# Two blocks of x turned on TensorE, thirds of queries taken in another order, and a rewritten order of work

## The chip, the cores and the metric

The kernel runs on one core of a Trainium2 chip. The core has TensorE (PE: matmuls and transposes; its weight loads, PEld, are shown apart), VectorE (DVE), ScalarE (ACT), GpSimd (POOL) and SyncE (SP), which here issues transfers. Each engine works through its own queue in order; engines meet through semaphores. The metric is the time of one execution in microseconds (us), taken as a median of several runs. Matmul results land in PSUM, which has eight banks of 2 KB per partition; they are copied or reduced from there by DVE or ACT.

## The reference

Attention in clusters is followed by a feed-forward layer, with 4 batches, 8 heads, 768 tokens, 64 numbers per head, and 16 centroids per head:

```python
q_assign = np.argmax(np.einsum('bhsd,hcd->bhsc', q_n, c_n), axis=-1)
k_assign = np.argmax(np.einsum('bhsd,hcd->bhsc', k_n, c_n), axis=-1)
mask = q_assign[:, :, :, None] == k_assign[:, :, None, :]
scores = np.where(mask, scale * np.matmul(q, k.transpose(0, 1, 3, 2)), -1e9)
attn = softmax(scores)
x = matmul(attn, v)              # then (B, S, H*D) -> 3072 tokens of 512
h = x @ w_in                     # 512 -> 1024
solu = h * softmax(h)
ln = (solu - mean) / sqrt(var + 1e-6) * g_ln
out = ln @ w_out                 # 1024 -> 512
```

## The kernel before

**First layer.** Work goes by pairs of heads (four pairs in each of four batches; a pair is written batch.pair). q and k of a pair are loaded and turned so that the head's numbers lie in partitions: in batch 0 by PE in fp32 (`turn_tokens`, L386, copied out by DVE or ACT at L393), later by DVE (L407). They are cast to bf16 into the pair's buffer `qk` (`cast`, L431 to L435). Centroid products (`clusters`, L445 and L450) are turned back by DVE (L459), the maximum taken (L472), the best cluster marked (L478, L484), turned (L491, L494), and the marks placed as further rows beside q and k (`place`, L506 to L514). So the score matmul adds a large constant where the clusters agree, and the exponential is taken with that constant as a shift: the mask costs no instruction.

A unit is two or three blocks of 128 queries of a head. Its scores fill three PSUM banks of 512 columns (two matmuls of 256 each, L601), or six narrower ones for pair 0.0; there are 294 banks in all and a ring of three buffers, `sps`. ACT takes the exponential of each bank into `e` (L607, nine buffers). Value matmuls (L624, six for each 128 queries) sum into one PSUM bank, `ops`. DVE divides by the sum of weights (the normalise, L636 and L649) and so writes x. There is one buffer of `ops`, so the value matmuls of a group wait for the normalise of the group before.

**Second layer.** It goes by blocks of 128 tokens, f = 0 to 23. x is turned into `xT` by a DMA transpose from SP (`turn_x`, L679), two blocks at a time in batches 0 to 2 (`turned`, L666) and one at a time after that; the last block is turned by PE into a buffer of the ring `sps` (`turn_x_pe`, L682) and copied out by DVE (`keep_x`, L690). Then PE makes h (L710, eight matmuls of 512 columns, written in four parts of two); DVE takes the negative maximum over 1024 columns (L716), ACT the exponential (L722) and DVE the product u (L727). u is turned (L732, by PE for the last two blocks), DVE takes its statistics (L738, L742), POOL makes the scale (L748 to L757), PE multiplies by w_out (L771), and ACT or DVE scales the result (L786, L788), which SP sends out (L798). One further PSUM bank, the pool `ps_m`, is passed along between the cluster products and the y of the blocks. An operation with `take="m"` waits for the `give="m"` of the one before it.

w_in comes in four loads of 512 KB (L549), each cast to bf16 by POOL (`cast_w_in`, L551; operations wi0 to wi3); h needs all four. w_out comes in four loads (L565), is multiplied by the gains and centred: weighted sums on PE (su0, su1: L574), a copy of them (sk: L581), a mean on PE (me: L584) and eight DVE instructions (L587).

**Order.** `Weave` (L16) holds all operations of a run with an engine, what they need and a cost. `ORDER` (L29 to L75) writes down for each engine the kinds of operations in sequence: S a bank of scores, E its exponential, V the values of a block, N a normalise, tp, xa, ca the turn, copy and cast of q or k, cl, tb, mx, oh, ot, pl the cluster steps, xt the turn by DVE, ld and lv loads, h, hm, ex, u, tu, bn, ag, at, al, y, sc, ou the steps of the second layer, tx the turn of x. The n-th token of a kind takes the n-th operation of that kind given to the engine; `AWAY` (L77) names operations moved from their usual engine to another. So the order in which each engine issues is fixed, and the chip's semaphores set the times.

`FIRST` (L280) is the order in which the pairs 1 to 3 of batch 0 are taken after pair 0, as (pair, third of the queries): (1,0) (1,1) (2,0) (2,1) (3,0) (3,1) and then the last third of each. The first two blocks of x need the first third of every pair.

## Time and profile before

| what | value |
|---|---|
| time, median of 3 runs | 225.78 us (225.64 to 225.80) |
| the profiled execution: time, span | 225.95 us, 223.9 us |
| PE, DVE, ACT, POOL busy | 215.1, 197.3, 191.5, 127.1 us |
| granted TensorE clock | 1.00 |
| chain that ended last | PE 86%, ACT 5%, DVE 3% |
| first h matmul, first maximum, first exponential of the second layer | 46.2, 49.0, 50.4 us |
| transposes of x by DMA, issue to landing (median) | 14, 3.2 us |
| loads of w_in, issue to landing (median) | 4, 5.9 us |

The span goes from the first to the last instruction; the rest of the time lies around it. A line of the timeline has start and duration in us, engine, line of the program, operation, output<-input, shapes and count; in brackets stands how long the engine was idle before it and what ended that. Matmuls overlap in a pipeline, so the distance from one start to the next, and not the duration, tells what one costs.

### The profile page before, as it was taken

The page shows a single profiled execution, that of the slowest core. Times are in us where ns is not written, and L with a number is a line of the kernel's source. Part 1 is how long each engine was busy: PE and PEld are TensorE (multiplying, and loading weights), DVE is VectorE, ACT ScalarE, POOL GpSimd, SP SyncE. Part 2 cuts the span into 40 slices and gives each one's busy share as a digit, 9 for nine tenths or more (in the row PEclk, how much of TensorE's full clock was granted, in tenths as well). Part 3 has the DMA queues.
Part 4 walks back from the last instruction along what each step waited for, and adds up shares of the span by engine and source line. Part 5 has one row for each costly group of instructions (what it writes and reads, how often), then busy time and mean ns, then how long its engine had stood idle before and what let it go on. Part 6 is the DMA issues. An engine that isn't in the chain of part 4 may idle for free.

```text
span 223.9 us, 6574 instructions
## 1 busy us (share of the span) xinstructions
PE 215.1 (96%) x2388; PEld 148.1 (66%) x2420; DVE 197.3 (88%) x359; ACT 191.5 (86%) x371; POOL 127.1 (57%) x247
## 2 busy tenths in 40 slices
PE   7899999999999999999999999999999999999993
PEld 3576756677667678776677667777677687754442
DVE  3799899899999989999998989887998889888981
ACT  3689999999998999998889899999999998982362
POOL 3489843964794999547668634943895413031331
PEclk9999999999999999999999999999999999999999
DMA  7998989999898989999999999199931433766622
GB/s 152 353 318 147 249 199 275 290 243 158 132 199 140 232 130 165 193 189 177 183 218 168 184 195 195 65 174 232 236 64 28 79 70 120 96 146 170 176 97 94
DMA packets 125679, 38.80 MB, mean 173 GB/s; under 512 B 115016, under 2 KB 121168, under 8 KB 125648
## 3 DMA queue, kind: packets, MB, share of 16 engines
q1 hardware_dynamic: 123904, 37.87, 80.6%
q10 hardware_dynamic: 1744, 0.52, 1.0%
q8 instruction: 19, 0.31, 0.6%
q14 instruction: 12, 0.10, 0.2%
HBM read 23.11 MB, written 6.29 MB: 131 GB/s over the span
## 4 chain that ended last, share of the span: by engine, by line
PE 86%; ACT 5%; DVE 3%; issue 3%; DMA 1%; POOL 1%; ACTq 0%; DVEq 0%; POOLq 0%
PE sps L601 28%; PE hreg L710 18%; PE yps L771 16%; PE ops L624 14%; ACT e L607 5%; PE csc L450 4%; PE hreg L386 2%; PE hreg L574 1%; PE hreg L771 1%; DMA c_all<-in_centroids_dram 1%; PE csc L445 1%; DVE bs L738 1%; DVE u L727 1%; ACT xt L393 0%; PE hreg L584 0%
## 5 line engine op out<-in xcount | busy, mean ns | idle before, releaser
L607 ACT ACTIVATE e<-sps 128x512 bf16<-128x512 f32 (+1 forms) x294 | 151.0, 599 | 12.2 <-PE sps L601 10.2
L601 PE MATMUL sps<-qk 80*128 80x256 bf16 (+5 forms) x636 | 93.8, 264 | 1.8 <-POOL qk L514 0.7
L601 PEld LDWEIGHTS <-qk 80*128 80x128 bf16 (+1 forms) x636 | 60.2, 121 | 27.9 <-issue 9.0
L624 PEld LDWEIGHTS <-e 128*128 128x128 bf16 x1152 | 50.4, 97 | 12.3 <-issue 1.9
L624 PE MATMUL ops<-v,e 128*128 128x65 bf16 x1152 | 55.0, 193 | 0.1
L710 PE MATMUL hreg<-w_in_sb,xT 128*128 128x512 bf16 x173 | 49.1, 379 | 1.1
L771 PE MATMUL yps<-w_out_c,uT 128*128 128x512 bf16 x171 | 46.4, 379 | 0.6
L727 DVE TENSOR_TENSOR u<-e_sb,hreg 128x1024 bf16<-128x1024 bf16 x24 | 29.0, 1210 | 4.9 <-ACT e_sb L722 4.7
L514 POOL COPY qk<-oht 32x384 f32<-32x384 f32 (+1 forms) x50 | 24.4, 488 | 15.8 <-DVE oht L494 13.6
L738 DVE BATCH_NORM_STATS2 bs<-u 128x6 f32<-128x512 bf16 x48 | 31.5, 676 | 0.2
L716 DVE TENSOR_REDUCE nmax<-hreg 128x1 f32<-128x1024 f32 x24 | 29.0, 1209 | 2.6 <-PE hreg L710 2.2
L722 ACT ACTIVATE e_sb<-hreg,nmax 128x1024 bf16<-128x1024 f32 x24 | 26.9, 1120 | 4.5 <-DVE nmax L716 4.4
L433 POOL CAST qk<-xt 64x768 bf16<-64x768 f32 (+1 forms) x31 | 26.1, 842 | 5.5 <-DVE xt L393 3.9
L771 PEld LDWEIGHTS <-uT 128*128 128x128 bf16 x200 | 18.2, 97 | 12.3 <-DVE uT L704 0.7
L754 POOL TENSOR_SCALAR esq<-es,mv 128x1 f32<-128x1 f32 x24 | 8.5, 355 | 29.0 <-DVE mv L742 20.8
L435 POOL TENSOR_SCALAR qk<-xt 64x768 bf16<-64x768 f32 (+1 forms) x28 | 23.0, 820 | 1.7
L710 PEld LDWEIGHTS <-xT 128*128 128x128 bf16 x192 | 16.8, 97 | 9.4 <-issue 0.6
L407 DVE STREAM_TRANSPOSE xt<-raw 128x768 f32<-128x768 f32 x24 | 22.6, 953 | 0.2 <-DMA raw<-in_q_dram 0.2
L748 POOL TENSOR_SCALAR es<-esum 128x1 f32<-128x1 f32 x24 | 5.3, 221 | 27.6 <-ACT e_sb L722 27.1
L649 DVE TENSOR_TENSOR x<-ops,den 128x256 bf16<-128x256 f32 (+1 forms) x39 | 18.9, 486 | 1.3
L757 POOL TENSOR_TENSOR alpha<-esq,halves 128x1 f32<-128x1 f32 x24 | 13.5, 561 | 2.0
L786 ACT ACTIVATE y<-yps,alpha 128x512 f32<-128x512 f32 x13 | 9.0, 692 | 6.4 <-PE yps L771 6.0
(80 smaller groups left out, 170.1 us busy)
## 6 DMA issues: line engine op xcount, KB each, us to landing
vf<-in_v_dram SPq DMA_DIRECT2D x16, 384.0 KB, 4.4
out_dram<-y SPq DMA_DIRECT2D x23, 256.0 KB, 2.7
raw<-in_q_dram SPq DMA_DIRECT2D x50, 96.0 KB, 3.7
raw<-in_k_dram SPq DMA_DIRECT2D x50, 96.0 KB, 3.0
w_g<-in_moe_w_out_dram SPq DMA_DIRECT2D x4, 512.0 KB, 5.3
w_st<-in_moe_w_in_dram SPq DMA_DIRECT2D x4, 512.0 KB, 5.9
raw<-in_q_dram SPq DMA_DIRECT2D x3, 384.0 KB, 6.3
raw<-in_k_dram SPq DMA_DIRECT2D x3, 384.0 KB, 6.8
```

The lines of the kernel that those rows point to most:

```text
L433: VEC[e].tensor_copy(dst, src)
L435: VEC[e].tensor_scalar(dst, src, scalar1=inv_C, scalar2=1.0, op0=Alu.mult, op1=Alu.mult)
L514: ins = VEC[e].tensor_copy(dst.bitcast(F32), src.bitcast(F32).unsqueeze(1) .to_broadcast([NB, 2, n // 2]))
L601: nc.tensor.matmul(sps_[n, k][:, c0:c0 + w], side(b, h // 2, 1, h % 2, keys)[r], side(b, h // 2, 0, h % 2, slice(s0 * P, s0 * P + w))[r])
L607: nc.scalar.activation(es[n, k][:, :w], sps_[n, k][:, :w], Act.Exp, scale=exp_scale, bias=-exp_scale)
L624: nc.tensor.matmul(opss[g][:, s, :VW], es[n, k][:, c0:c0 + P], v1[slot(b, h // 2)][:, h % 2, kt, :VW], start=(kt == 0), stop=(kt == n_t - 1))
L710: uses(nc.tensor.matmul(hreg[:, at(f, f2)[1], :], xTs[f][:, dc, :], w_in_sb[:, dc, f2 * FF2:(f2 + 1) * FF2], start=(dc == 0), stop=(dc == ...
L716: uses(nc.vector.tensor_reduce(ff[f, "nmax"][:], pair_of(f), axis=AXY, op=Alu.max, negate=True), *both(f))
L722: uses(nc.scalar.activation(ff[f, "e"][:], pair_of(f), Act.Exp, bias=ff[f, "nmax"][:], accum_out=ff[f, "esum"][:]), *both(f))
L727: uses(nc.vector.tensor_tensor(ff[f, "u"][:], ff[f, "e"][:], pair_of(f), op=Alu.mult), *both(f))
L738: nc.vector.bn_stats(ff[f, "bs"][:, f2, :], ff[f, "u"][:, f2, :])
L771: ins = nc.tensor.matmul(dst, ff[f, "uT"][:, at(f, f2)[0] * (n_fc // 2) + c, :], w_out_c[:, fc, cols], start=(fc == 0), stop=(fc == n_fc - 1))
```

## The change

- x of blocks 0 and 1 is turned by PE, each block for itself: four transposes into the `ps_m` bank (operations ptx0 and ptx1) and a copy out by DVE (tx0, tx1). Their DMA transpose goes; `turned` now pairs blocks from 2 on.
- `FIRST` takes the first thirds of pairs 2 and 3 ahead of their second thirds, so that pair 3 begins two units sooner.
- The order of every engine is written anew, and some operations change engines. In the front: wi0 goes from POOL to DVE; sk from DVE to ACT; the clearing of the marks' rows (zo) and one blanking from DVE to POOL; copies, casts and placings of pairs 0 to 3 are exchanged between DVE, ACT and POOL. On SP the v loads of pairs 1 and 2 go ahead of k of pair 2, the first w_out loads come earlier, and the w_in loads go ahead of the last three loads of k of pair 1.1.

The diff, with only the first rows of the orders:

```diff
     ORDER["SP"] = """
-        ld4 lv si ld4 lv lg ld4 lv2 ld4 lo2 ld4 lo ld3 lo ld3 li4 tx ld3 lv3 tx ld4 tu ld9 lv ld tu
+        ld4 lv si ld3 lv2 ld2 lg ld4 lo ld lo ld5 lv ld lo ld3 lo li4 ld7 lv3 ld5 tx ld tu ld5 lv2
...
     ORDER["POOL"] = """
-        po z ca2 pl2 cv z bl pl2 ca z ca pl2 ca z2 ca3 cv ca cv ca pl3 sg ca cv2 pl3 ca2 gs pl ca cv
-        ca wi ca pl2 wi3 bl ca pl2 cv at cv pl ca pl al bl at cv ca pl ca pl cv ca3 al at ca al ca
+        po ca3 pl2 bl pl2 zo bl cv ca2 pl sg cv ca2 cv pl3 ca z gs pl3 ca4 z3 ca pl2 cv3 ca2 wi3 pl2
+        ca pl2 cv bl ca at pl cv pl2 cv2 pl bl al ca cv ca4 at z al at2 pl4 al ca2 bl ca2 cv al pl2
...
     ORDER["PE"] = """
-        wm tp2 cp tp cl tp fl5 cl fl4 S3 tp2 S2 tp S cq S tp S2 tp2 S2 V3 S cl S tp2 V3 S gt S tp S
-        tp S2 cl S2 V2 S V S2 tp S2 tp S2 V2 S V S2 cl S2 V2 S V2 S3 V S2 V2 S2 V S cl S3 su S2 V3 S
-        V S3 V3 S2 V S su S2 V S V3 S3 me S3 V4 S3 cl S3 V4 S2 h S h S2 h S h S2 V3 S2 V h S h V S V
+        wm tp2 cp tp cl tp fl5 cl fl4 S3 tp cq S2 tp S2 tp S2 tp S tp S V S V2 cl tp S2 V3 S tp2 S
+        tp S gt S tp S2 cl S V3 S3 tp S tp S2 V3 S2 cl V S3 su S2 V3 S3 cl S V S2 V S V2 S3 V2 S V2
+        S4 V S V S V2 S su S3 me S2 V2 S2 ptx V2 S2 ptx S V S V2 S V S h S h S2 V h S2 V2 S cl S V S
...
     ORDER["DVE"] = """
-        cn cb xa ca tb mx oh ot pl2 tb mx oh ot xa3 bl cf cv xa zo xa2 tb ca mx oh gk N ot tb pl mx
-        xa2 oh xa cv N ot tb pl N xt mx xt N oh ot tb pl2 ca N pl xt mx N sk oh N ot xt ce3 N tb ce5
-        N hm mx N u oh ot bn N bn ag hm xt2 u N bn2 hm ag sc xt u N bn tb hm mx bn oh ag u xt bn ot
+        cn xa2 cb tb mx oh ot pl2 tb mx oh ot cf ca pl xa3 cv xa ca xa tb mx oh ot xa2 gk N cv tb mx
+        oh ot xa pl N ca xt tb xt pl mx N oh ot pl2 N tb mx ca N oh xt wi N ot ce2 tx N ce tx xt N
+        ce5 tb N hm mx N u bn2 oh N ot xt ag hm xt2 u N bn hm bn cv tb ag u N mx oh ot hm bn2 xt u N
...
     ORDER["ACT"] = """
-        wa xa2 ca2 xa ca2 E12 xa2 E6 xa E58 ex E12 ex E8 ex E8 ex E3 sc E5 ca E2 ex E25 ex E9 sc E6
+        wa xa2 ca4 E12 xa E5 xa E4 xa E5 xa E26 sk E23 ex E14 ex E4 sc E3 ex E10 ex E8 ex sc E11 sc
...
-    FIRST = [(p, s) for p in range(1, n_pair) for s in range(2)] + [(p, 2) for p in range(1, n_pair)]
+    FIRST = [(1, 0), (1, 1), (2, 0), (3, 0), (2, 1), (3, 1), (1, 2), (2, 2), (3, 2)]
...
     def turned(f):
 
-        return list(range(f - f % 2, f - f % 2 + 2)) if f < (B - 1) * n_t else [f]
+        return list(range(f - f % 2, f - f % 2 + 2)) if 2 <= f < (B - 1) * n_t else [f]
...
     def turn_x_pe(f):
         b, su = divmod(f, n_t)
         take_x(f)
-        ff[f, "xp"] = ps_s.tile([P, n_dc, P], BF16, name="xtp", tag="sps")
+        ff[f, "xp"] = ((ps_m if f < 2 else ps_s)
+                       .tile([P, n_dc, P], BF16, name="xtp", tag="m" if f < 2 else "sps"))
...
-    def keep_x(f):
-        nc.vector.tensor_copy(xTs[f], ff[f, "xp"][:])
+    def keep_x(f, e="DVE"):
+        (nc.scalar.copy if e == "ACT" else nc.vector.tensor_copy)(xTs[f], ff[f, "xp"][:])
...
+            elif f < 2:
+                add(f"ptx{f}", "PE", 0.24, s, (lambda e, f=f: turn_x_pe(f)), nd, take="m")
+                add(f"tx{f}", "DVE", 0.36, s - 2, (lambda e, f=f: keep_x(f, e)), [f"ptx{f}"],
+                    give="m", also={"ACT": 0.5})
             else:
                 add(f"tx{f}", "SP", 1.28, s, (lambda e, f=f: turn_x(f)), nd,
-                    [f"tx{x_turns[-1]}"] if x_turns else [], move=0.65 * len(fs), lag=(0.1, 0.7))
+                    [f"tx{x_turns[-1]}"] if x_turns[2:] else [], move=0.65 * len(fs), lag=(0.1, 0.7))
```

More of the change, by code (lines that the diff above doesn't have):

```diff
@@ L68 @@
+        u oh mx bn N bn bl ot cv xt2 N hm ca ag ca u N cv bl cv hm oh sc u bn2 ot tb hm mx N ag oh
+        bn u ot bn N hm sc ag u bn2 N hm bn N u ag hm N u bn2 hm sc bn N u ag2 bn2 hm ag N bn u hm N
+        bn u hm ag bn4 u N bn ag hm tx ag sc u bn ag bn hm bn ag tu u bn2 tu ag sc2
     """
     ORDER["ACT"] = """
[L70 to L71 removed]
```

66 lines of the change are left out of this document (31 added, 35 removed).

## The prediction

> **What bounds the kernel now.** I read, in this order, the page's busy line and its chain, the sums by stretch of time for the first 60 us, and the timeline around three places that the change touches.
>
> The page, busy line and chain:
>
> ```profile
> PE 215.1 (96%) x2388; PEld 148.1 (66%) x2420; DVE 197.3 (88%) x359; ACT 191.5 (86%) x371; POOL 127.1 (57%) x247
> ...
> PE 86%; ACT 5%; DVE 3%; issue 3%; DMA 1%; POOL 1%; ACTq 0%; DVEq 0%; POOLq 0%
> ```
>
> TensorE (PE) sets the end, but its busy time holds the tails of pipelined matmuls. So I priced PE by distances from start to start in the timeline: a bank of scores 0.219 us, a group of six value matmuls 0.192, a pair of 512-wide matmuls (h, L710, or y, L771) 0.431, a pair's cluster scores 0.78, three fp32 turns 0.33. 270 score banks (59.1) and the 24 narrow ones (4.0), 192 value groups (36.9), 96 h (41.4), 96 y (41.4), 17 cluster products (12.6), 16 groups of turns (5.3) and the rest, warm-up included (8.3), make 208.9 us. The span is 223.9: the first matmul starts at 1.2, the last result leaves PE 3.6 before the end, and 10.6 us are gaps on PE. By starts, 3.1 of them lie before 20 us, 3.6 between 20 and 60, 2.6 between 60 and 200 and 1.3 in the tail.
>
> Sums by stretch (columns: PE, PE weight loads, DVE, ACT, POOL busy; clock; DMA share; GB/s):
>
> ```profile
> 20.00:25.00 5.00, 4.71 (x66) 3.40 (x66) 4.67 (x11) 4.89 (x12) 4.62 (x10) 1.00 0.74 214
> 25.00:30.00 5.00, 4.89 (x77) 3.46 (x70) 4.34 (x8) 4.84 (x11) 4.00 (x8) 1.00 0.82 163
> 30.00:35.00 5.00, 4.88 (x62) 2.67 (x59) 4.80 (x11) 4.65 (x10) 2.48 (x4) 1.00 1.07 241
> 35.00:40.00 5.00, 4.93 (x74) 3.27 (x74) 4.18 (x10) 4.59 (x10) 0.86 (x2) 1.00 0.91 283
> 40.00:45.00 5.00, 4.89 (x56) 3.12 (x56) 4.55 (x10) 4.70 (x10) 4.85 (x7) 1.00 1.19 280
> 45.00:50.00 5.00, 4.94 (x69) 3.82 (x68) 4.82 (x9) 5.00 (x11) 3.31 (x6) 1.00 1.24 261
> ```
>
> The reader sees that the front is not bound by one engine: PE, DVE and ACT are each over 90% full, so a wait on any of them soon reaches the others. DVE's idle time from 20 to 50 is 30 - 27.4 = 2.6 us. This front is what the change reorders; after 60 us there is little left to win.
>
> The timeline at the first weights cast, the first maximum and the first exponential of the second layer, and PE behind them:
>
> ```profile
> 39.59 1.04 POOL L552 CAST w_in_sb<-w_st 128x1024 bf16<-128x1024 f32 x1 [4.13 <-DMA w_st<-in_moe_w_in_dram]
> ...
> 46.16 0.60 PE L710 MATMUL hreg<-w_in_sb,xT 128*128 128x512 bf16 x2
> ...
> 48.98 1.22 DVE L716 TENSOR_REDUCE nmax<-hreg 128x1 f32<-128x1024 f32 x1
> ...
> 50.36 1.11 ACT L722 ACTIVATE e_sb<-hreg,nmax 128x1024 bf16<-128x1024 f32 x1
> ...
> 52.11 0.38 PE L601 MATMUL sps<-qk 80*128 80x256 bf16 x2 [0.26 <-ACT e L607]
> ```
>
> The first weight cast waited for its load; the last of the four ended at 45.6, and h began at 46.2. The first maximum ended at 50.20, the exponential went at 50.36 and held ACT 1.1 us, and PE waited behind it for a free score bank.
>
> **The change part by part.** The sum is made against the profiled execution: span 223.9, time 225.95, so 2.05 lie around the span; it is 0.17 above the median of 225.78.
>
> (1) Two blocks of x turned by PE. Eight more matmuls. The trace has four of this kind:
>
> ```profile
> 207.53 0.39 PE L688 MATMUL xtp<-ident_b,x 128*128 128x128 bf16 x4
> 207.76 0.59 PE L710 MATMUL hreg<-w_in_sb,xT 128*128 128x512 bf16 x2
> ```
>
> Four start 0.23 apart from the next work: 2 x 0.23 = **+0.46** of PE, on the path, since PE is the bound. The copies out are two more DVE instructions of 0.41 (L691's row).
> The Trainium skill (TensorE: Matmul & The Clock Gate, Part 4) puts one such transpose at about 275 ns in a kernel's context. By it the eight would cost 2.2 instead of 0.46; the row disagrees, with 219 ns each but overlapped, so the sum keeps 0.46.
>
> (2) The transfer that goes. SP waited 2.6 us in it (37.61 to 40.21, for a normalise) and issued for 1.34; all loads behind it move up. On the path it gives 0: h waits for the weight casts (45.6), while a transpose issued at 40.2 lands in the median 3.2 later. If that cover went, it could give the 0.6 between the last cast and h. The weight loads also stand three loads earlier on SP (issued from 33.72 before; the place is now 31.23), so the first lands at 37.1 if the latency of 5.9 holds, or at 38.1 if the bandwidth does.
>
> (3) DVE up to the first maximum, where the work is moved between engines. Added: two whole casts of q (0.74 each, L433) less one of k (0.52), one weight cast, two copies of x (0.82). Gone: the sum's copy (0.69, now on ACT), two memsets (0.63). Transposed pair halves, v casts and placings exchange one for one. The weight cast on DVE has no row; below it lies the 128x512 copy (0.69), above it 1024/384 of the v cast of 0.43 (1.14); I take 0.95, in line with the 768-wide cast at 0.74. Net 0.96 + 0.95 + 0.82 - 0.69 - 0.63 = **+1.4 us** of DVE ahead of the first maximum. DVE has 2.6 idle there. Bounds: all absorbed and some idle time recovered, -1.0; nothing absorbed, +1.4. The value I take is **+0.4**: most of the idle time is broken into pieces of 0.2 to 0.4, so about 1.0 of it can be filled.
>
> (4) New waits on DVE. The weight cast now stands ahead of the normalise of pair 3, so DVE stops until the first weights land (37.1 to 38.1); by the rows DVE comes to it at about 37.7 (the normalise before it went at 34.70, plus 0.9 of added work, 0.7 for itself, 0.5 and 0.9 for the two instructions between). That is a wait of 0 to 0.4, part of the +0.4 above. Behind it wait the normalise, which frees the only bank of values' sums for the next value group, then the copies of x. The second turn waits for the first copy, as both use the one spare PSUM bank: PE has 1.05 us of other work between, the copy takes 0.41 and two handoffs, so it costs nothing unless DVE is late.
> The Trainium skill (Perfetto Trace Analysis, Matmuls) asks for independent matmul groups to rotate through PSUM banks, so that evacuation overlaps; the turns do not. By it this would be a stall; by the rows it becomes one only through DVE's delay, which is counted.
>
> (5) The exponential. The first one stands one score bank earlier on ACT than before. If the maximum is late by d, it starts at 50.25 + d, the next score exponential ends at 51.95 + d and the second at 52.45 + d; PE then waits at the second bank after. PE's work ahead of that bank is 45.1 us (44.5 at the wait of 52.11 before, which had 7.6 us of gaps and start behind it, growing to 7.8 soon after). So the gaps there become 7.4 + d instead of 7.8: **-0.4 + d = 0** for d = 0.4. The gaps gained ahead of it (the places of pair 1 now before other POOL work: scores waited 0.6 for them at 22.16; the first scores some 0.3 earlier) are swallowed by this wait, which is late next.
>
> (6) Thirds taken earlier. Pair 3's casts and places are needed two units (six banks, some 3 us) earlier. Their last cast ended at 33.8 and PE reached that place at 31.3. In the new order three casts and three tiny memsets (2.6 us) separate pair 2's last cast from it on POOL, against 2.9 of PE work: cost 0, bounds -0.3 and +1.0. Its loads are moved too: v of pairs 1 and 2 now goes ahead of k of pair 2 (issued at 5.45 before, 6.8 to landing by the page's median, turned only at 15.9). Two loads of 384 KB at the 353 GB/s of the second slice put it 2.2 later, at about 14.5, still ahead of its turn.
>
> (7) After 60 us DVE has +1.3 more (casts and v casts against y scalings), ACT two more scalings and one cast less (+0.5). Between 60 and 200 DVE idles 11.5 of 140, ACT 9.9: no cost. POOL has less work. The tail holds the same PE work after the last scores. Cost 0, bounds -0.5 and +1.5.
>
> Sum: 225.95 + 0.46 + 0.0 = 226.4 profiled, 226.3 as a median.
>
> **The rivals.**
> A. Faster: DVE fills its idle time, the maximum starts at or before 48.6, and the 3.6 us of gaps from 20 to 60 shrink. For it: h can begin four score banks earlier, with a cluster product and the weight sums moved into stretches where PE ran ahead of ACT. Against: the second weight sum still needs the last w_out load, and h the last of the w_in loads, which allow at most about 1.0 to 1.5. With -1.0 from DVE and 0.3 to 0.9 from gaps ahead: 225.78 + 0.46 - 1.3 to 1.9, about 224.6. It decides where the maximum is over 0.5 us earlier than mine.
> B. Slower by the weight cast: if the first w_in tile still lands at 39.5, as before, DVE stands 2 us, the normalise ends at 40.9, PE stops 1.3 before the next value groups, and d grows to 1.3: 225.78 + 0.46 + 0.9 = 227.1.
> C. A stall that the order brings later, between 60 and 200, where DVE is 98 to 99% full in single stretches (60 to 70, 90 to 100, 110 to 120): 227.5 with 1.2 of it.
> D. The turns do not overlap near 40 us as they did at 207.5, each paying its full 219 ns: 8 x 0.219 = 1.75, so 227.5. For it: they stand alone between score matmuls; against it: so did the four of the row. (By the Trainium skill's 275 ns, in the section named above, it would be 228.0.)
>
> **How the numbers follow.** Mine 0.42 (225.7 to 226.9), A 0.28, B 0.15, C 0.12, D 0.03. The predicted time is 226.3. Within 0.2% (0.45 us) nothing can be told from no change here: 225.33 to 226.23 is the same. Of mine 0.22 falls there and 0.20 above; of A 0.26 below and 0.02 in it; B, C and D are above. So faster 0.26, same 0.24, slower 0.50. The range goes from 224.4 (within A) to 228.0 (C with its bound of 1.5 and B's lower delay); it leaves out A's fast end and the slow ends of B and C, under 0.2.
>
> **What would show it.** Step 1: eight rows of L688's kind near 40 us, four in 0.23. Step 4: a DVE cast of w_st with idle time before it that ends in its load. Step 5: the first maximum near 49.4, and PE's wait for ACT behind the first exponential. Steps 6 and 7: no new PE gap before pair 3's scores nor after 60 us. I am wrong if the maximum stands over 0.5 us off, or if PE's gaps after 60 us change by more than 1 us.

## The result, and the profile after

The changed kernel takes 228.74 us (median of four executions, 228.05 to 229.40) where the kernel before takes 225.79 (225.64 to 226.15) beside it: a ratio of 1.0129, 95% interval 1.0101 to 1.0158. It is slower by 2.9 us. The prediction had the sign, as the likelier side, but 226.3 is 2.4 too low, and 228.74 lies 0.7 above its range. Here and below a ratio is of the fast executions alone (those not over 1.5% above the fastest of their kernel), so it is not the quotient of the medians beside it.

The profiled execution took 228.05, 2.10 above the 225.95 of before; its span is 226.3 where it was 223.9. The page of the changed kernel, busy line and chain:

```profile
PE 218.6 (97%) x2428; PEld 148.7 (66%) x2428; DVE 200.3 (89%) x364; ACT 193.0 (85%) x373; POOL 122.4 (54%) x237
...
PE 84%; DVE 6%; POOL 3%; issue 2%; DMA 1%; ACT 1%; SPq 0%; DVEq 0%; POOLq 0%
```

TensorE is still what ends last, but DVE's part of the chain went from 3% to 6%, and POOL's from 1% to 3%: waits for these two have come into TensorE's path.

The sums by stretch of the changed kernel (columns as before):

```profile
25.00:30.00 5.00, 4.96 (x64) 2.47 (x56) 4.87 (x10) 4.64 (x10) 4.62 (x9) 1.00 1.05 254
30.00:35.00 5.00, 4.51 (x76) 3.40 (x69) 4.79 (x10) 4.83 (x10) 2.91 (x6) 1.00 0.74 248
35.00:40.00 5.00, 4.78 (x52) 2.82 (x50) 3.66 (x9) 4.86 (x11) 4.45 (x5) 1.00 1.05 336
```

From 30 to 35 us TensorE idles 0.5 where it idled 0.1; DVE is full up to 35 (4.87 where it was 4.34, then 4.79) and stands idle after that (3.66 of 5).

The timeline of the changed kernel at that place, then at the turns, then at the first maximum and the first exponential:

```profile
30.87 0.98 DVE L491 STREAM_TRANSPOSE w_out_c<-w_out_c 128x768 bf16<-128x768 bf16 x1
...
31.89 0.93 DVE L506 COPY qk<-w_out_c 16x384 f32<-16x384 f32 x2
31.98 1.20 POOL L506 COPY qk<-w_out_c 16x384 f32<-16x384 f32 x2 [2.05 <-DVE w_out_c L491]
...
32.09 0.38 PE L601 MATMUL sps<-qk 80*128 80x256 bf16 x2
...
32.96 0.49 PE L601 MATMUL sps<-qk 80*128 80x256 bf16 x3 [0.49 <-ACT e L607]
```

The bank at 32.96 is the first of pair 3. It starts 0.87 after the bank before it, of which 0.22 is work. The profile names ACT, but the second of DVE's two copies (32.27 to 32.82), which places pair 3's marks, ended later than the exponential did (32.42). So the marks are taken as the last input here; the trace does not name them. DVE reached these copies only after the marks were turned, at 31.85.

```profile
37.05 0.65 DVE L552 CAST w_in_sb<-w_st 128x1024 bf16<-128x1024 f32 x1
...
41.63 0.39 PE L689 MATMUL xtp<-ident_b,x 128*128 128x128 bf16 x4
42.05 0.42 DVE L692 COPY xT<-xtp 128x512 bf16<-128x512 bf16 x1
...
42.67 0.39 PE L689 MATMUL xtp<-ident_b,x 128*128 128x128 bf16 x4
43.65 0.42 DVE L692 COPY xT<-xtp 128x512 bf16<-128x512 bf16 x1
...
44.61 0.59 PE L711 MATMUL hreg<-w_in_sb,xT 128*128 128x512 bf16 x2
```

```profile
49.32 0.59 PE L711 MATMUL hreg<-w_in_sb,xT 128*128 128x512 bf16 x2
...
50.02 1.22 DVE L717 TENSOR_REDUCE nmax<-hreg 128x1 f32<-128x1024 f32 x1
...
51.34 1.11 ACT L723 ACTIVATE e_sb<-hreg,nmax 128x1024 bf16<-128x1024 f32 x1
```

The weights' cast on DVE has no wait; the next matmuls start 0.22 to 0.23 behind each group of turns; h begins 1.55 earlier than before. Yet the first maximum is 1.04 later (50.02; 48.98 before): it waits for the last part of h, whose matmuls end at 49.91, not for DVE.

**Where the 2.10 lies.** I put TensorE's work at the prediction's prices in the order of its queue and call the *lag* of a matmul its start less the work ahead of it: the sum of all gaps and of the start, 11.8 us at the end before and 13.2 after. The growth of the lag by stretch of work (work of 25 to 35 us is done between about 31 and 43 us of time), worked out from the timelines:

```
work, us         to 5   5-25  25-35  35-60  60-150  150-155  155-end   all
before           2.70   3.26   0.91   1.15    1.80     0.11     1.86  11.78
after            2.76   3.12   1.89   0.97    2.15     0.30     2.05  13.24
after_again      2.58   3.12   2.31   0.97    2.11     0.27     2.05  13.42
after_third      3.94   2.98   2.67   1.04    2.10     0.92     2.03  15.68
```

Of the 2.10, 0.45 is the turns' matmuls and 1.46 is lag: 1.0 between 25 and 35, 0.35 between 60 and 150, 0.2 each in the two last columns, and -0.2 between 35 and 60. Added up to 60 us of work that is 0.72 (8.74 where it was 8.02), and 0.73 behind it. The last 0.2 lie outside TensorE's work: 0.4 more between the last matmul and the end of the span, 0.2 less around the span. The other executions of the changed kernel are slower than the profiled one by 0.5 to 1.4, which one profile cannot explain; the two later ones (runs below) show more in three of the columns, to 5, 25-35 and 150-155. The first of the three is the start of the kernel:

```profile
6.43 0.87 PE L386 MATMUL hreg<-ident_f,raw 128*128 128x128 f32 x3 [0.64 <-DMA raw<-in_q_dram]
```

That is the third profile (after_third), where a load of q landed at 6.29 and not at 5.70 as in the first. No run was made on this start; it is 1.2 of what the third profile has over the first.

### The profile page after: what moved, and what is told of

Read it like the earlier page. It is cut to its first block, busy times and chain, and to the rows that moved or that the text cites. A ratio compares the mean times of both kernels' runs of the same rounds, so it can differ in the third digit from the quotient of the medians.

```text
span 226.3 us, 6617 instructions
## 1 busy us (share of the span) xinstructions
PE 218.6 (97%) x2428; PEld 148.7 (66%) x2428; DVE 200.3 (89%) x364; ACT 193.0 (85%) x373; POOL 122.4 (54%) x237
## 3 DMA queue, kind: packets, MB, share of 16 engines
HBM read 23.11 MB, written 6.29 MB: 130 GB/s over the span
## 4 chain that ended last, share of the span: by engine, by line
PE 84%; DVE 6%; POOL 3%; issue 2%; DMA 1%; ACT 1%; SPq 0%; DVEq 0%; POOLq 0%
PE sps L601 27%; PE hreg L711 18%; PE yps L772 16%; PE ops L624 15%; PE csc L450 4%; DMA raw<-in_k_dram 1%; PE hreg L386 1%; ACT e L607 1%; DVE xt L393 1%; PE hreg L574 1%; PE hreg L772 1%; POOL qk L435 1%; POOL qk L514 1%; DVE oh L484 1%; PE csc L445 1%
## 5 line engine op out<-in xcount | busy, mean ns | idle before, releaser
L601 PE MATMUL sps<-qk 80*128 80x256 bf16 (+5 forms) x636 | 95.2, 264 | 1.7 <-POOL qk L514 0.7
L711 PE MATMUL hreg<-w_in_sb,xT 128*128 128x512 bf16 x192 | 52.8, 379 | 0.0
L772 PE MATMUL yps<-w_out_c,uT 128*128 128x512 bf16 x184 | 47.6, 379 | 0.1
L514 POOL COPY qk<-oht 32x384 f32<-32x384 f32 (+1 forms) x44 | 21.5, 489 | 22.2 <-DVE oht L494 18.1
L435 POOL TENSOR_SCALAR qk<-xt 64x768 bf16<-64x768 f32 (+1 forms) x30 | 25.9, 862 | 2.6 <-DVE xt L393 0.8
L433 POOL CAST qk<-xt 64x768 bf16<-64x768 f32 (+1 forms) x24 | 19.7, 821 | 4.2 <-DVE xt L393 2.1
L749 POOL TENSOR_SCALAR es<-esum 128x1 f32<-128x1 f32 x24 | 6.7, 286 | 18.0 <-ACT e_sb L723 17.5
L787 ACT ACTIVATE y<-yps,alpha 128x512 f32<-128x512 f32 x15 | 10.5, 700 | 6.8 <-PE yps L772 6.6
L532 POOL CAST v<-vf 128x384 bf16<-128x384 f32 x24 | 12.2, 519 | 4.8 <-DMA vf<-in_v_dram 4.1
```

Of the source, the lines that this page charges most:

```text
L435: VEC[e].tensor_scalar(dst, src, scalar1=inv_C, scalar2=1.0, op0=Alu.mult, op1=Alu.mult)
L514: ins = VEC[e].tensor_copy(dst.bitcast(F32), src.bitcast(F32).unsqueeze(1) .to_broadcast([NB, 2, n // 2]))
L601: nc.tensor.matmul(sps_[n, k][:, c0:c0 + w], side(b, h // 2, 1, h % 2, keys)[r], side(b, h // 2, 0, h % 2, slice(s0 * P, s0 * P + w))[r])
L711: uses(nc.tensor.matmul(hreg[:, at(f, f2)[1], :], xTs[f][:, dc, :], w_in_sb[:, dc, f2 * FF2:(f2 + 1) * FF2], start=(dc == 0), stop=(dc == ...
L772: ins = nc.tensor.matmul(dst, ff[f, "uT"][:, at(f, f2)[0] * (n_fc // 2) + c, :], w_out_c[:, fc, cols], start=(fc == 0), stop=(fc == n_fc - 1))
```

## The experiments

Each ran beside the kernel before on the same chip.

**1. The two halves, the turns alone, and the same again.** For the halves, every queue takes one kernel's order up to 60 us of its timeline and the other's remaining instructions, in their order and on their engines; the first rows that differ, on SP:

```diff
 # front of before, later order of the change (front_before; FIRST and the turns as before)
-        ld4 lv si ld4 lv lg ld4 lv2 ld4 lo2 ld4 lo ld3 lo ld3 li4 tx ld3 lv3 tx ld4 tu ld9 lv ld tu
+        ld4 lv si ld4 lv lg ld4 lv2 ld4 lo2 ld4 lo ld3 lo ld3 li4 tx ld3 lv3 tx ld4 tu ld8 lv2 ld3
...
 # front of the change, later order of before (front_after; FIRST and the turns as changed)
-        ld4 lv si ld3 lv2 ld2 lg ld4 lo ld lo ld5 lv ld lo ld3 lo li4 ld7 lv3 ld5 tx ld tu ld5 lv2
+        ld4 lv si ld3 lv2 ld2 lg ld4 lo ld lo ld5 lv ld lo ld3 lo li4 ld7 lv3 ld5 tx ld tu ld5 lv
...
 # turns_alone: the kernel before, new code of turned, turn_x_pe and keep_x, no tx on SP; PE and DVE:
-        V S3 V3 S2 V S su S2 V S V3 S3 me S3 V4 S3 cl S3 V4 S2 h S h S2 h S h S2 V3 S2 V h S h V S V
+        V S3 V3 S2 V S su S2 V S V3 S3 me S3 ptx V4 ptx S3 cl S3 V4 S2 h S h S2 h S h S2 V3 S2 V h S
...
-        xa2 oh xa cv N ot tb pl N xt mx xt N oh ot tb pl2 ca N pl xt mx N sk oh N ot xt ce3 N tb ce5
+        xa2 oh xa cv N ot tb pl N xt mx xt N oh ot tb pl2 ca N pl xt mx N sk oh N ot tx xt tx ce3 N
```

> The changed kernel unchanged, for its spread and a second profile. In the first comparison its four times went from 228.05 to 229.40 (1.35 us), those of the kernel before from 225.64 to 226.15. Theory P (a fixed set of waits, the same in each execution): the second profile has the wait of 0.65 ahead of pair 3's scores at 32.1, the first maximum at 50.0, and the time is 228.0 to 228.9. Theory V (some waits come and go with the landing of transfers): the second profile has a time 0.5 us or more from 228.05, and the difference stands in gaps of TensorE that the first profile does not have, each behind a load.

> Up to 60 us the order, the turns and the thirds of the kernel before; from there on the order and the engines of the changed kernel. The two profiles put the 2.1 us between them as 0.45 of work for the turns and 0.2 of gaps before 60 us, 0.7 of gaps between 60 and 200, and some 0.5 more behind the last matmuls. Theory L (the later order costs by itself): 226.9 to 227.6. Theory F (the front is late, and the later order only shows it): 225.6 to 226.2.

> Up to 60 us the changed kernel, turns on TensorE and thirds included; from there on the order and the engines of the kernel before. Theory L: only the front's 0.65 is left, 226.3 to 226.7. Theory F: 228.0 or more, as the changed kernel. If both this and the kernel with the front of before are slower by about half each, costs add up by place.

> The kernel before with one thing changed: x of blocks 0 and 1 turned on TensorE at 42 us and copied out by VectorE behind the last normalise, and no transpose by DMA for them. By my step 1: +0.46, so 226.2. If h then starts earlier, as SyncE's loads move up by 1.3 us of issue: 225.6 to 225.8. If the turns do not overlap with other matmuls (219 ns each): 227.5.

Before 225.53 here. The changed kernel again: 229.02 (228.22 to 230.47), ratio 1.0130 (1.0085 to 1.0176). front_before: 228.39, 1.0123 (1.0068 to 1.0179). front_after: 228.33, 1.0101 (1.0067 to 1.0135). turns_alone: 226.92, 1.0054 (1.0028 to 1.0080).

The second profile of the changed kernel took 228.22 and has the 0.65 ahead of pair 3 again, as theory P says; it has one more wait, 0.55, which stands behind DVE and not behind a load (below).

Of the halves neither L nor F holds: each alone seems to cost nearly the whole. The lags tell why. In its one profile each hybrid has a wait at its seam that neither parent has: 1.83 ahead of a y that starts at 69.8 us and waits for the landing of its u, and 1.29 ahead of an h that starts at 63.3 and waits for DVE's u. Without it the columns are within 0.4 of those of the parents:

```
work, us         to 5   5-25  25-35  35-60  60-150  150-155  155-end   all
front_before     2.16   3.25   0.91   1.37    3.96     0.27     2.04  13.96
front_after      3.01   2.79   2.31   2.64    1.79     0.13     1.87  14.53
```

The later order costs its 0.3 to 0.4 in the column 60-150 and its 0.2 in the last, whatever the front; the front costs its 1.0 to 1.4 in 25-35, whatever comes later. So two losses, both of the order itself, as far as one profile of each hybrid can tell.

turns_alone gave +1.39 where step 1 said 0.46. Its timeline shows what I had placed wrongly:

```profile
41.86 0.43 DVE L693 COPY xT<-xtp 128x512 bf16<-128x512 bf16 x1 [1.51 <-PE xtp L690]
...
46.05 0.92 PE L625 MATMUL ops<-v,e 128*128 128x65 bf16 x24 [0.90 <-DVE x L650]
```

DVE came to the copy 1.5 us before TensorE came to the turn; everything behind it on DVE was late, the normalise too, and TensorE waited. That is a cost of the place; turns_later, below, separates it from that of the turn.

**2. One suspect each.** The copy of the sums back on DVE; a normalise ahead of a cast; the turns placed without a wait; the change without the turns.

```diff
 # sk_on_dve: on the changed kernel, DVE and ACT
-        oh ot xa pl N ca xt tb xt pl mx N oh ot pl2 N tb mx ca N oh xt wi N ot ce2 tx N ce tx xt N
+        oh ot xa pl N ca xt tb xt pl mx N oh ot pl2 N tb mx ca N oh xt wi N sk ot ce2 tx N ce tx xt
...
-        wa xa2 ca4 E12 xa E5 xa E4 xa E5 xa E26 sk E23 ex E14 ex E4 sc E3 ex E10 ex E8 ex sc E11 sc
+        wa xa2 ca4 E12 xa E5 xa E4 xa E5 xa E49 ex E14 ex E4 sc E3 ex E10 ex E8 ex sc E11 sc E13 ex
...
 # normalise_first: on the changed kernel, DVE
-        oh ot xa pl N ca xt tb xt pl mx N oh ot pl2 N tb mx ca N oh xt wi N ot ce2 tx N ce tx xt N
+        oh ot xa pl N ca xt tb xt pl mx N oh ot pl2 N tb mx N ca oh xt wi N ot ce2 tx N ce tx xt N
...
 # turns_later: the kernel before with the turns, placed otherwise; PE and DVE
-        V S3 V3 S2 V S su S2 V S V3 S3 me S3 V4 S3 cl S3 V4 S2 h S h S2 h S h S2 V3 S2 V h S h V S V
+        V S3 V3 S2 V S su S2 V S V3 S3 me ptx S3 V3 ptx V S3 cl S3 V4 S2 h S h S2 h S h S2 V3 S2 V h
...
-        xa2 oh xa cv N ot tb pl N xt mx xt N oh ot tb pl2 ca N pl xt mx N sk oh N ot xt ce3 N tb ce5
+        xa2 oh xa cv N ot tb pl N xt mx xt N oh ot tb pl2 ca N pl xt mx N sk oh N ot xt tx ce2 tx N
...
 # no_turns: the changed kernel with the old code of turned; no ptx, no tx on DVE; SP
-        ld4 lv si ld3 lv2 ld2 lg ld4 lo ld lo ld5 lv ld lo ld3 lo li4 ld7 lv3 ld5 tx ld tu ld5 lv2
+        ld4 lv si ld3 lv2 ld2 lg ld4 lo ld lo ld5 lv ld lo ld3 lo li4 ld4 tx ld3 lv3 ld5 tx ld tu
```

> The changed kernel with the copy of the weighted sums (sk) back on VectorE, right behind the normalise at 38.2, where VectorE then stood idle for 1.8 us; ScalarE has 0.5 less. Theory A (from 31 us to the first exponential ScalarE is the bound: it idled 0.5 of 18 us there): the first exponential comes 0.5 earlier, at about 50.8, and the time falls by 0.4 to 0.5, to 228.2 to 228.5 against 228.7 to 229.0. Theory D (VectorE is the bound of the front, as my step 3 had it): no gain, or 0.3 to 0.7 slower.

> The changed kernel with the normalise of the third group of 34.7 us ahead of VectorE's cast of k, instead of behind it. In two of three profiles that cast took 1.25 us and GpSimd's cast of the same tile, begun 0.02 us away, 0.82; in the third it was 0.55 and 1.22. Theory R (the two casts race for something that only one of them can hold; when VectorE loses, the normalise is late and TensorE waits 0.55 ahead of the value matmuls): here that wait is gone however the casts end, the lag of TensorE after it is 0.3 to 0.5 smaller, and the times are 228.0 to 228.6 with a smaller spread than 1.3 us. Rival (the cast is only late because of its data, or ScalarE sets the pace anyway): time and lag as before, 228.7 to 229.0.

> The kernel before with x of blocks 0 and 1 turned on TensorE as in the run with the turns alone, but the turns two and one group earlier on TensorE and the copies one to three instructions later on VectorE, so that no copy waits for its turn (there VectorE stood 1.5 us at the first copy, and TensorE 1.06 for the next normalise). Theory W (the turns cost their 0.46 and all else was that wait): 226.0 (225.9 to 226.2, against 225.5 without and 226.9 with the wait). Rival (the turns cost 1.4 wherever they stand, by the copies' 0.8 on VectorE): 226.8 to 227.0.

> The changed kernel without the turns on TensorE: x of blocks 0 and 1 goes by one DMA transpose again, issued behind the first load of k of pair 1.2. All else as in the changed kernel. Theory P (TensorE is the bound there too, the turns' matmuls lie on the path): 0.46 less, 228.2 to 228.5. Theory A (ScalarE sets the pace up to the first exponential): 0 to 0.2 less. Theory T (the transfer cannot be hidden in this order, its landing holds up h, and that is what the turns were worth): slower than the changed kernel by 0.5 or more.

The kernel before took 226.47 here and varied more (225.54 to 229.46). sk_on_dve: 229.02, 1.0103 (1.0055 to 1.0151). normalise_first: 229.99, 1.0137 (1.0085 to 1.0189). turns_later: 226.02, 0.9995 (0.9969 to 1.0022). no_turns: 231.15, 1.0190 (1.0136 to 1.0244).

- sk: its column 35-60 is 0.98, as in the changed kernel, and no time was won. Theory A (ScalarE) falls for this place, which lies behind the waits of 25-35.
- The turns without a wait: no cost that can be told from none. Repeated:

> The kernel before with the turns on TensorE placed so that nothing waits, once more, on another chip or at another time. The first run gave 226.02 against 226.47, in a call where the kernel before went from 225.5 to 229.5. If the turns cost their 0.46 of TensorE's time and nothing else: 0.4 to 0.5 above the kernel before where that is at 225.5. If the transfer that goes was a source of late executions: a median at or below that of the kernel before, and a narrower spread.

It measured 225.76 against 225.61, 1.0014 (0.9990 to 1.0038). The lag in 35-60 is 1.03 there against 1.15, so a part of the 0.45 of matmuls seems to be paid back where the transfer went. Four turns start 0.23 ahead of the next work, and the copy follows them at once:

```profile
40.63 0.39 PE L690 MATMUL xtp<-ident_b,x 128*128 128x128 bf16 x4
40.86 0.82 PE L602 MATMUL sps<-qk 80*128 80x256 bf16 x6
41.06 0.42 DVE L693 COPY xT<-xtp 128x512 bf16<-128x512 bf16 x1
```

- Without the turns the changed order takes 231.15 where sk_on_dve, beside it, takes 229.02 (theory T): the DMA transpose, issued at 42.21, landed at 45.47 and h waited 0.5 for it, and the transpose of blocks 2 and 3 behind it was issued only at 54.06. So the turns are not what costs; in this order they save.
- normalise_first: the wait ahead of the value matmuls at 35 us was gone, as theory R says (25-35 is 1.89, as in the first profile), but the time did not fall. The profile shows other losses in its place: 0.44 and 0.81 ahead of two parts of h of block 2, of which the first waited for its transpose and the second for DVE's u, and 0.92 in 150-155.

**The race.** The 1.89 or 2.31 to 2.67 of the column 25-35 comes from one pair of casts of the same tile, one on DVE and one on POOL. The timeline of the changed kernel in its first profile, and in the second:

```profile
34.58 0.56 DVE L433 CAST qk<-xt 64x768 bf16<-64x768 f32 x1
34.60 1.22 POOL L433 CAST qk<-xt 64x768 bf16<-64x768 f32 x1
```

```profile
34.40 1.25 DVE L433 CAST qk<-xt 64x768 bf16<-64x768 f32 x1
34.42 0.82 POOL L433 CAST qk<-xt 64x768 bf16<-64x768 f32 x1
```

They start 0.02 apart, DVE first in both. Either DVE takes 0.56 and POOL 1.22, or DVE 1.25 and POOL 0.82: one goes ahead and the other is longer by nearly the length of the first. With the changed front and this cast in its place DVE won in two profiles (after, thirds_back) and lost in six (after_again, after_third, front_after, sk_on_dve, no_turns, tx2_early). The cast is no new one: in the kernel before it stands on DVE too, but begins 0.28 ahead of POOL's, and in all seven profiles with that front the two take 0.74 and 1.15:

```profile
34.03 0.74 DVE L433 CAST qk<-xt 64x768 bf16<-64x768 f32 x1
34.31 1.15 POOL L433 CAST qk<-xt 64x768 bf16<-64x768 f32 x1
```

When DVE loses, the normalise behind its cast ends at 36.2 instead of 35.7, and TensorE waits 0.55 by its starts (second profile):

```profile
36.26 0.36 PE L624 MATMUL ops<-v,e 128*128 128x65 bf16 x6 [0.39 <-DVE x L649]
```

The same pair of lengths is found at 158 us, between a v cast on DVE and a cast on POOL; the first profile, and the third (after_third, below):

```profile
158.29 1.04 POOL L435 TENSOR_SCALAR qk<-xt 64x768 bf16<-64x768 f32 x1
158.30 0.35 DVE L532 CAST v<-vf 128x384 bf16<-128x384 f32 x1
...
160.75 1.11 ACT L723 ACTIVATE e_sb<-hreg,nmax 128x1024 bf16<-128x1024 f32 x1 [0.18 <-DVE nmax L717]
```

```profile
160.12 0.83 POOL L435 TENSOR_SCALAR qk<-xt 64x768 bf16<-64x768 f32 x1
160.14 1.02 DVE L532 CAST v<-vf 128x384 bf16<-128x384 f32 x1
...
163.20 1.11 ACT L723 ACTIVATE e_sb<-hreg,nmax 128x1024 bf16<-128x1024 f32 x1 [0.80 <-DVE nmax L717]
...
164.94 0.27 PE L601 MATMUL sps<-qk 80*128 80x256 bf16 x1 [0.59 <-ACT e L607]
```

Where the v cast takes 1.02, the maximum behind it comes 0.62 later, ACT idles 0.80 for it, and TensorE 0.75 ahead of the next scores: the column 150-155 is 0.92 instead of 0.30. The Trainium skill (SBUF — State Buffer, section "SBUF: two separate sides") says that DVE, in some of its instructions, and GpSimd take a shared pair of ports as an exclusive lock, and that whichever starts first holds it for its whole instruction. The traces agree with one holder and a loser that stands still, but for 0.1: in both orders the two casts of k have ended 1.25 after the start, where such a cast takes 0.54 on DVE with nothing on POOL beside it (125.3 us, first profile) and 0.82 on POOL, 1.36 together. Which of two that start 0.02 apart holds it, they show to be open.

**3. Undo the thirds, and mend single waits.**

```diff
 # thirds_back: on the changed kernel
-    FIRST = [(1, 0), (1, 1), (2, 0), (3, 0), (2, 1), (3, 1), (1, 2), (2, 2), (3, 2)]
+    FIRST = [(p, s) for p in range(1, n_pair) for s in range(2)] + [(p, 2) for p in range(1, n_pair)]
...
-        S4 V S V S V2 S su S3 me S2 V2 S2 ptx V2 S2 ptx S V S V2 S V S h S h S2 V h S2 V2 S cl S V S
+        S4 V S V S V2 S su S3 me S2 V2 S2 V2 S3 V ptx S V2 S V ptx S h S h S2 V h S2 V2 S cl S V S h
...
 # mended: normalise_first's row, POOL's bl four places forward, the two v casts behind hm and oh
-        at ca2 cv ca5 pl ca pl at cv pl al cv bl cv al pl4 cv pl ca at2 ca3 al pl2 at2 al cv2 ca cv
+        at ca2 cv ca5 pl ca pl at bl cv pl al cv2 al pl4 cv pl ca at2 ca3 al pl2 at2 al cv2 ca cv bl
...
-        u oh mx bn N bn bl ot cv xt2 N hm ca ag ca u N cv bl cv hm oh sc u bn2 ot tb hm mx N ag oh
+        u oh mx bn N bn bl ot cv xt2 N hm ca ag ca u N bl hm oh cv2 sc u bn2 ot tb hm mx N ag oh bn
```

> The changed kernel unchanged, on the chip of the next three, as their reference and for a third profile. Theory R (its spread comes from casts that race between VectorE and GpSimd, and from the landing of the third transpose of x): VectorE's v cast at 158 us (0.35 in two profiles) and its cast of k at 34.5 (0.55 or 1.25) take one of two durations each, and TensorE's wait ahead of the scores 76.1 at 163 us is 0.75 where the v cast took 1.0 and none where it took 0.35. The time is 228.2 to 229.5 where the kernel before takes 225.5 to 226.5.

> The changed kernel with three instructions moved: the two v casts on VectorE at 158 us go behind the maximum and the mark that follow (GpSimd idles from 160.4 to 165.0 there, so nothing can race), the normalise at 35 us goes ahead of the cast of k that races, and GpSimd's blanking ahead of pair 2.3's scores goes three places forward. Theory R and the places' waits: TensorE's lag is smaller by 0.3 at 140 us (the wait of 0.31 ahead of the scores 65.0 goes), has no jump at 163 us in any execution, and the time is 0.3 to 1.2 below that of the changed kernel, by how often it loses the races, with less spread. Rival (the waits are only moved on to the next engine): the same time within 0.3, and other gaps in their place.

> The changed kernel with the thirds of queries in the order of the kernel before (pair 3 two units later), the turns some 2 us later on TensorE as x is ready later, and all other tokens where they were. Theory P (the wait of 0.65 ahead of pair 3's first scores at 32 us and the 0.4 to 0.55 behind it are the price of taking thirds early, step 6): those gaps go, the lag at 60 us is smaller by 0.7 to 1.0, and the time with it. Theory A (ScalarE had no idle time there from 31 us on, so TensorE only ran ahead and would wait at the next score bank): the gaps move to other banks, lag and time as in the changed kernel within 0.2. Theory H (x ready later delays the first h and with it the maximum): slower by 0.3 to 1.

Before 225.61. The changed kernel 229.04 (227.87 to 233.17), 1.0135 (1.0094 to 1.0176). mended: 229.03, 1.0136 (1.0102 to 1.0170). thirds_back: 228.75, 1.0140 (1.0109 to 1.0171).

- thirds_back has no wait ahead of pair 3; it has 0.44 ahead of value matmuls and 0.27 + 0.38 at the ring instead, and its column 25-35 is 2.38, though DVE won its cast. The time stays. So the order of thirds decides where the wait stands, and taking it back does not shorten it (theory A).
- mended: the time stayed (229.03 against 229.04), and so did the spread, as the rival said. The column 150-155 falls to 0.19, as theory R says. The wait of 0.31 ahead of scores 65.0 went, and 0.40 came ahead of value matmuls in the same column: 60-150 stays 2.09. In the front nothing was won in this execution, because a load of k of pair 1.0 landed at 28.3 instead of 24.4, and DVE, whose next instruction turns it, idled 1.35 (5-25 is 4.28, 25-35 2.06).

**4. Take casts off DVE, put one on, and move the third transpose of x.**

```diff
 # casts_back: on the changed kernel, ca0.3.0.0 and ca1.0.0.1 on POOL (two_mends: and the v casts as in mended)
-        po ca3 pl2 bl pl2 zo bl cv ca2 pl sg cv ca2 cv pl3 ca z gs pl3 ca4 z3 ca pl2 cv3 ca2 wi3 pl2
+        po ca3 pl2 bl pl2 zo bl cv ca2 pl sg cv ca2 cv pl3 ca z gs pl3 ca5 z3 ca pl2 cv3 ca3 wi3 pl2
...
 # cast_added: on the kernel before, ca0.3.0.0 on DVE
-        xa2 oh xa cv N ot tb pl N xt mx xt N oh ot tb pl2 ca N pl xt mx N sk oh N ot xt ce3 N tb ce5
+        xa2 oh xa cv N ca ot tb pl N xt mx xt N oh ot tb pl2 ca N pl xt mx N sk oh N ot xt ce3 N tb
...
 # zo_early: on the kernel before, zo from DVE to POOL
-        po z ca2 pl2 cv z bl pl2 ca z ca pl2 ca z2 ca3 cv ca cv ca pl3 sg ca cv2 pl3 ca2 gs pl ca cv
+        po zo z ca2 pl2 cv z bl pl2 ca z ca pl2 ca z2 ca3 cv ca cv ca pl3 sg ca cv2 pl3 ca2 gs pl ca
...
 # tx2_early: on the changed kernel, SP (three_mends: and two_mends)
-        ld4 lv si ld3 lv2 ld2 lg ld4 lo ld lo ld5 lv ld lo ld3 lo li4 ld7 lv3 ld5 tx ld tu ld5 lv2
+        ld4 lv si ld3 lv2 ld2 lg ld4 lo ld lo ld5 lv ld lo ld3 lo li4 ld7 lv3 tx ld6 tu ld5 lv2 ld3
```

> The changed kernel with two casts of q and k (0.95 at 25.6 us and 0.55 or 1.25 at 34.6) back from VectorE to GpSimd, which idles there from 29.9 to 32.0. Theory D (VectorE's work sets the front from 20 to 36 us): the fifth normalise ends 1.0 to 1.5 earlier, at 34.2 to 34.7, TensorE's lag at 60 us is 0.7 to 1.2 smaller, and the time about 228.0 where the changed kernel had 228.7 to 229.0 in three calls. Rival (loads, or the ring of scores with ScalarE, hold the front): the normalise waits for its value matmuls instead, lag and time within 0.3 of the changed kernel.

> The same, and the two v casts at 158 us behind the maximum and the mark, so that nothing races there. By theory D and the race: 227.3 to 227.9, no jump of the lag at 163 us, and a spread below 1.3 us. By the rivals: 228.4 to 229.0.

> The kernel before with one thing moved: the first cast of q of pair 3 goes from GpSimd to VectorE behind the normalise at 24.9 us, as in the changed kernel, 0.55 to 0.95 of work. Theory D: the fifth normalise ends 0.5 to 0.9 later than 35.3, and the time rises by 0.3 to 0.9 (some of it absorbed in VectorE's idle pieces of 1.05 in all from 20 to 35 us). Rival (VectorE is not the bound; GpSimd has 0.8 to 1.2 less to do, so the places of the pairs come earlier): the same time or 0.2 to 0.4 faster.

> The kernel before with one thing moved: the clearing of the marks' rows, 0.38 on VectorE at 14.5 us, goes to GpSimd's start, where GpSimd idles from 3.5 to 7.5. Theory D: VectorE's chain runs 0.2 to 0.4 earlier from 15 us on, and the time falls by 0.1 to 0.4, which would beat both kernels. Rival: no change, within 0.1.

Before 225.74. casts_back: 229.19, 1.0135 (1.0100 to 1.0170). two_mends: 228.31 (227.27 to 229.19), 1.0096 (1.0060 to 1.0132). cast_added: 226.27, 0.9990 (0.9959 to 1.0022). zo_early: 225.87, 0.9987 (0.9963 to 1.0011).

```
work, us         to 5   5-25  25-35  35-60  60-150  150-155  155-end   all
casts_back       3.66   2.91   1.64   2.68    2.19     0.46     2.05  15.59
two_mends        2.92   2.91   1.64   1.99    2.10     0.18     2.04  13.79
cast_added       2.37   3.25   0.91   1.15    2.66     0.11     1.87  12.32
zo_early         2.75   2.91   0.91   1.15    2.01     0.11     1.86  11.70
```

In the kernel before, 0.4 to 0.5 more or less of DVE's work changes no column from 25 to 60, and up to 25 the kernel with more and the one with less are alike (5.62 and 5.66): there DVE is not the bound, and theory D falls for it (what cast_added has in 60-150 is 0.75 at a y at 101 us whose transpose of u landed late). In the changed kernel, two casts less on DVE bring the column 25-35 from 1.89 to 2.67 down to 1.64, and both waits, ahead of pair 3 and ahead of the value matmuls, are gone. What is left are three waits of 0.27 for exponentials at the ring. So of the 1.0 that the first profile lost here, the two casts account for 0.25; the 0.4 and 0.8 more of the second and third, where DVE loses the race, go as well. Yet casts_back gained no time. Its profiled execution lost 0.9 more at the start (3.66), and h of block 2 waited for its input:

```profile
54.30 1.35 SPq L679 DMA_TRANSPOSE xT<-x  x1
...
56.22 0.38 PE L601 MATMUL sps<-qk 80*128 80x256 bf16 x2
...
57.82 0.39 PE L711 MATMUL hreg<-w_in_sb,xT 128*128 128x512 bf16 x1 [1.22 <-DMA xT<-x]
```

This transpose (blocks 2 and 3) was issued at 45.2 in the kernel before. The changed order puts five loads ahead of it, and in nine profiles it was issued between 49.1 and 54.3; from 52.6 on, TensorE waits, 0.2 to 1.4. The three profiles of the changed kernel itself (49.1 to 50.8) have no such wait.

> The changed kernel with one token moved on SyncE: the transpose of x of blocks 2 and 3 stands right behind the v loads of pairs 1.0 to 1.2, as in the kernel before, and no longer behind five more loads. Theory T (its landing is late in some executions, and h of block 2 waits): it is issued at 45.5 to 47.5 us and lands before 53 us, TensorE has no gap over 0.3 ahead of the first h of block 2 (it had 0.2 to 1.4), and the median falls by 0.3 to 0.7, to 228.2 to 228.6. Rival (the five loads behind it are what is late then): gaps ahead of pair 1.2's scores or at 58 to 62 us instead, and the same 228.7 to 229.0.

> The changed kernel with that transpose moved, the two casts of q and k back on GpSimd, and the two v casts at 158 us behind the maximum and the mark. If the three losses are separate and add: 227.2 to 227.8, with no gap over 0.3 between 30 and 60 us except the ring's, and a lag of TensorE at the end within 0.9 of the kernel before. What is left then is the turns' 0.2 to 0.5 and the later order's 0.6. If each mend only hands the wait on: 228.3 (as with two of them) or more.

Before 225.93. tx2_early: 228.26 (228.03 to 229.80), 1.0107 (1.0052 to 1.0162). three_mends: 227.60 (226.99 to 230.29, 12 executions), 1.0078 (1.0043 to 1.0113). With all three the timeline of three_mends reads:

```profile
45.43 1.53 SPq L679 DMA_TRANSPOSE xT<-x  x1
47.06 5.16 SPq L399 DMA_DIRECT2D raw<-in_k_dram  x4
...
55.55 0.60 PE L711 MATMUL hreg<-w_in_sb,xT 128*128 128x512 bf16 x2
```

The transpose goes at 45.4, and the four loads that had stood ahead of it take 5.2 us to issue. h of block 2 (55.55) starts 0.22 after the bank before it, without a wait. The lag at the end is 12.73: 0.73 above before in 25-35, 0.4 in 60-150, 0.25 behind that, less 0.5 before 25 and between 35 and 60. Three small moves (one transfer, two pairs of casts), with the turns and the order of thirds left as changed, so took back 1.4 of the 3.2 us between the medians of the changed kernel (229.0) and the kernel before (225.8). By the ratios it is 1.2 us, and the interval of 1.0078 just overlaps those of the changed kernel, which did not run on this chip; what each move gives by itself the intervals do not separate. No kernel of these is shown to beat the kernel before; zo_early and turns_later cannot be told from it.

**Open.** What holds the remaining 0.7 in 25-35 is open: the waits are for exponentials, and ACT is busier there than it was (in the changed kernel 4.83 and 4.86 of 5 from 30 to 40 us, before 4.65 and 4.59), but no run took work off ACT ahead of 31 us. So are the late start of some executions (3.66 and 3.94 in the first column) and the 0.3 to 0.4 in 60-150, which moved to the next wait when its largest single wait was mended.

## Why the prediction was wrong

The step that failed is the front's net cost of 0.0, which steps 3, 5 and 6 made together. In the prediction's terms, step 5 took d, the lateness of the first maximum, to be what DVE was late (0.4), and step 6 put the wait ahead of pair 3 at nothing. The runs show d = 1.0, which came from TensorE: h was late by waits that stood ahead of pair 3's scores and behind them.

- **Step 1, the turns: right.** Two rows of four, each 0.22 ahead of the next work; alone and well placed they cost 0.15 in time at the second measurement and nothing at the first (by the intervals up to 0.9 and 0.5). Rival D falls: eight times 219 ns is not paid. So does the Trainium skill's 275 ns (TensorE: Matmul & The Clock Gate, Part 4), by which the eight would cost an estimated 2.2: the row has 0.22 for four. This 0.46 was all that made the forecast a slower kernel, and the time hardly shows it. The sign came out by other losses, which was luck.
- **Step 4, the weights' cast: right in size, the wait was none.** The first load landed at 34.97, ahead of the 37.1 that I took; the cast took 0.65, not 0.95. Rival B falls.
- **Step 3, "net +1.4 us of DVE ... the value I take is +0.4": right for DVE, but only where it wins a race.** At the end of the fifth normalise DVE had done 29.9 us where it had done 28.4, 1.5 more; 1.1 of it went into idle time ahead of that place, and the normalise ended 0.36 late (35.68; 35.32 before), 0.88 in the second profile. What the step had wrong is that a cast has one price: it takes 0.56 or 1.25, by what POOL does beside it.
- **Step 6, "cost 0, bounds -0.3 and +1.0": failed at its upper bound,** 0.65 ahead of pair 3 and 0.38 behind it. I had looked at the casts, the last inputs in the kernel before; in the new order the last input is the placing of the marks, at the end of a chain on DVE. Taking the thirds back does not help, and two casts off DVE take these waits away but leave 0.7 of the column at the ring. What holds the 0.7 stays open.
- **Step 5, the maximum at 49.4: 50.02, d = 1.0.** It waited for TensorE, not for DVE. The gaps ahead of it were not "swallowed by this wait": the last part of h started 0.97 later than before, 0.73 of it by lag and 0.24 by more work ahead of it. The step's rule held: by 7.4 + d the gaps would be 0.6 larger, and up to 60 us of work the lag is 0.72 larger.
- **Step 7, "cost 0, bounds -0.5 and +1.5": failed inside its bounds.** 0.3 to 0.4 in 60-150, 0.2 at the end, and the race at 158 us, 0.2 or 0.8. That is half of the first profile's added lag. Rival C had this, but alone.
- **A step that was missing.** The transpose of blocks 2 and 3 goes behind five loads on SP. I followed the loads that the change moves up, and not what stands behind them. It costs 0 to 1.4 us of TensorE's time, different in each execution; in the three profiles of the changed kernel itself it costs 0.

The prediction's account of TensorE's span has one reading that is off: the last matmul ends 3.3 ahead of the end of the span, not 3.6, so its parts add up to 0.4 too much. No later step uses it.

With what the runs show, the sum is 225.95 + 0.45 (turns) + 1.0 to 1.8 (25-35) + 0.35 + 0.2 to 0.8 + 0.2 (later) + 0 to 1.4 (transpose), less 0.2 to 0.4 regained elsewhere: 227.8 to 230.8; the three profiled executions took 228.05, 228.22 and 230.48. The third is not reached by these terms as its profile has them (no wait for the transpose): 1.2 of it is the late start. Rival A, a faster front, found nothing: the h that began 1.55 earlier ended later.

## What to carry to other kernels

When an order is rewritten, count an engine's added work up to the first place that waits for it, and set against it only the idle time ahead of that place. Then ask the same of every other engine: the maximum here waited for TensorE, which had been made late by two others. Two engines that cast the same tile at the same moment had two results here, so a written order that brings such pairs together has a spread and not a time; look for instructions of one kind whose length takes two values. For each queue list also what now stands *behind* the moved transfers: a transpose that is five loads later looks harmless at 4 us of slack and is the first to be late.

## What was not expected of the hardware

- A cast on DVE and one on POOL, begun 0.02 us apart, overlap by about 0.1 us only: 0.56 and 1.22 or 1.25 and 0.82 us (64x768), 0.35 and 1.04 or 1.02 and 0.83 (v, 128x384). Both results occur with the same program, and which engine's record starts first does not tell the winner: in the first pair it is DVE's in both, in the second POOL's.
- Even the cast of w_in on POOL took 1.54 us instead of 1.04 where DVE cast another part of w_in beside it, with both begun within 0.01 us of each other.
- Four loads of 96 KB took 5.2 us to issue on SP at 47 us, where others take 0.5 each; one of the four took 3.2. What held them the runs do not show; what stands behind such loads is late with them.
